# Retention and a gated MLP in one kernel: q loaded four tokens to a partition, w_in as float32 by SyncE's queue, an engine listed per cast

## The chip, the cores and the metric

One core of a Trainium2 chip. TensorE (PE) multiplies and writes to PSUM, VectorE (DVE), ScalarE (ACT) and GpSimd (POOL) do the elementwise work, SyncE (SP) issues transfers between HBM and SBUF, which run on the core's 16 DMA engines. The metric is the device time of one execution in microseconds (us), lower is better. A profiled execution has in addition a span: from the first to the last instruction that the profile shows.

## The reference

Eight batches, eight heads, 576 positions, head size 64. Retention (attention without softmax, with a decay for each head), then an MLP over the 512 joined features whose V half is normed, mixed over positions by a 576 x 576 matrix and multiplied onto the U half:

```python
scores = scale * np.matmul(q, k.transpose(0, 1, 3, 2))
gamma = 1.0 - 2.0 ** (-5.0 - np.arange(H))
Dmat = np.where(rel >= 0, gamma[:, None, None] ** rel[None, :, :], 0.0)
x = np.matmul(scores * Dmat, v)          # (B, H, S, D), then joined to (B, S, 512)

h = gelu_tanh(x @ w_in)                  # w_in: 512 x 1024
u, v = h[..., :512], h[..., 512:]
v_n = (v - mean(v)) / np.sqrt(var(v) + 1e-06) * g_ln
v_s = np.einsum('ts,bsd->btd', w_sg, v_n) + b_sg[None, :, None]
return x + (u * v_s) @ w_out
```

Everything enters and leaves as float32; the kernel multiplies in bfloat16.

## The kernel before

Two batches make a pair p of 1152 tokens. For attention a pair is nine tiles n (`U = 9`, 36 in all): four heads by 256 tokens of one batch each, but for the middle one (`MID` = 4), which holds all heads of 64 tokens of each batch. For the MLP a pair is nine tiles m of 128 tokens.

A tile of attention goes so. `load` (line 311) brings its q, k and v as float32 into one of six buffers (`qkf`, `vf`), by SyncE's queue, 256 KB a load; a row of SBUF gets two neighbouring tokens of each head, so 512 bytes run together in HBM. The middle tile takes two loads of 128 KB for each of q, k and v. `scaled` (504) casts k to `kb`, multiplies q by the decay into `qs` and v by its inverse into `vb`, all bfloat16. `turned` (541) transposes q and k on PE (8 matmuls, L547) and copies them from PSUM to `qkT`. `score` (566, L572) multiplies q by k, `mask` (576) puts the triangle on and writes `ret`; `states` (596, L605) multiplies k by v into running states, which `keep` (626) adds up in float32 (`s1`, `s2`, `zmid`) and casts to `zsA` and `zsB`. `outp` (678, L692) adds the products of q with the states and of `ret` with v, and writes `xT`, features by tokens. For tiles from the twentieth on, q and k are transposed by DMA (L499).

The MLP takes `xT`: `mlp_V` (815, L821, 4 matmuls of 512 columns) needs the V half of `w_in`, its gelu and statistics follow, then `norm` writes `vn`; `mlp_U` (857, L868) needs the U half. `batch` (878) does the mixing with w_sg (L890), the product with U (L898) and the out projection (L923), which adds x by identity matmuls (L926) or, in the last 18 tiles, from a DMA transpose.

`w_load` (338) brings `w_in` in four pieces, each half of the rows by half of the columns, through GpSimd's own queue; that DMA casts to bfloat16 on the way. It stands in GpSimd's program between its casts and products. The first two pieces are V's, the others U's. `weights` (447) loads w_sg, casts it on GpSimd, transposes it on PE and copies it to `wT` (and, shifted by 64 partitions, `wT1`); `w_out` follows.

The order of the whole program is a list: the table `TURN` holds for every unit of work (by the name of what it writes, in the order of `plan.add`) its place, and `Plan.emit` issues the units in that order, each on its engine. An engine runs its instructions in that order and waits at each for what it needs. `Plan.emit` reckons times from each unit's `cost` for two things only: which PSUM bank a unit takes, and where PE is given matmuls on zeros (`fill`, L301) to keep it busy, up to 45 us. Transfers of SyncE's queue take turns at eight semaphores, and each waits until the one eight earlier has landed.

Of the kernel before, what the change touches and what calls it, by code (L numbers as in the profile page):

```python
# [11 lines left out]
F32 = mybir.dt.float32  # L12
# [7 lines left out]
    "b_col": [57],  # L20
    "b_rows": [0, 58],
    "b_tr": [72],
    "dtab": [33],
# [4 lines left out]
    "g_col": [76],  # L28
    "g_col1": [89],
    "g_inv": [90],  # L30
    "g_rows": [21, 109],
    "g_tr": [121],
    "gelu": [51],
# [6 lines left out]
    "ident": [4],  # L40
# [12 lines left out]
    "otu": [48, 55, 92, 110, 136, 162, 197, 268, 304, 335, 377, 419, 447, 472, 498, 539, 554, 582, 610, 640, 673,  # L53
        703, 718, 751, 782, 823, 839, 883, 914, 946, 969, 1004, 1026, 1053, 1068, 1101],
# [32 lines left out]
        807, 810, 945, 922, 940, 928, 1019, 1065, 1046, 1044, 1066, 1143, 1120, 1149, 1147],  # L87
    "wT": [244, 247, 273, 239, 276],
    "wT1": [326, 327, 293, 370, 287],
    "wT_b": [74],  # L90
    "wTp": [238, 237, 272, 233, 275],
    "w_in": [25, 38, 100, 82],
    "w_out": [320, 298, 333, 331],
# [923 lines left out]
```

## Time and profile before

| | us |
|---|---|
| median of 3 runs | 209.04 (207.84 to 210.18) |
| the profiled execution | 209.62 |
| its span | 207.9 |
| first U product of w_in (L868) starts | 29.33 |
| first mixing product (L890) starts | 50.38 |
| last matmul ends | 203.1 |

The page gives busy time by engine, the span in 40 slices, DMA queues, the chain of work that ended last, and groups of instructions by line. `out<-in` names the tiles; "128*128" is the part of PE's array in use, "128x512" partitions by elements. In a timeline each row is a start, a length, the engine, and in brackets how long the engine sat idle before it and what it waited for. SyncE's loads keep the DMA engines busy nearly all the time: over the span they moved 48.20 MB in 98321 packets, 90.0% of 16 engines' span on SyncE's queue and 3.6% on GpSimd's.

### The profile page before, as it was taken

Reading aid. Unit: us, or ns where it says so; the run is one execution under the profiler, and the core shown is the slowest. Engines: PE = TensorE matmul, PEld = TensorE weight load, DVE = VectorE, ACT = ScalarE, POOL = GpSimd, SP = SyncE. Lnnn points to the kernel's source line nnn. Section 1 sums busy time; section 2 is a strip of 40 time slices with the busy share of each in tenths; the row PEclk is TensorE's granted clock in tenths of the full one; section 3 lists DMA queues with packets and bytes.
Section 4 is the critical chain, followed back from the end, with each engine's and each line's share of the span. In section 5 each row is a group of like instructions: output and inputs, shape, how many; then the busy total and the mean of one; then the engine's idle time right before and its main releaser. Section 6 shows DMA issues by size and latency. Waiting matters only on the chain.

```text
span 207.9 us, 7429 instructions
## 1 busy us (share of the span) xinstructions
PE 194.2 (93%) x2994; PEld 124.2 (60%) x3027; DVE 150.8 (73%) x366; ACT 134.7 (65%) x316; POOL 135.8 (65%) x231
## 2 busy tenths in 40 slices
PE   6977949999999999999999999999999999999992
PEld 2543536768767776567745666575656565664651
DVE  1654953998987888978786658575869689896672
ACT  5363325799999846788589776765777377826400
POOL 6557989489769996759779865749846866123200
PEclk9999966999999999999999999999999999999999
DMA  5999999999999998695999899998998999895815
GB/s 145 267 203 192 228 274 302 300 296 309 192 277 251 290 330 213 175 241 136 265 210 299 229 175 199 271 317 208 255 267 236 201 175 262 192 189 195 249 54 202
DMA packets 98321, 48.20 MB, mean 232 GB/s; under 512 B 42288, under 2 KB 92720, under 8 KB 98288
## 3 DMA queue, kind: packets, MB, share of 16 engines
q1 hardware_dynamic: 97056, 46.56, 90.0%
q0 software_dynamic: 1088, 1.05, 3.6%
q8 instruction: 23, 0.38, 0.8%
q10 hardware_dynamic: 144, 0.13, 0.2%
q14 instruction: 10, 0.08, 0.1%
HBM read 32.79 MB, written 9.44 MB: 203 GB/s over the span
## 4 chain that ended last, share of the span: by engine, by line
PE 85%; DMA 8%; POOL 2%; issue 2%; DVE 1%; SPq 0%; DVEq 0%; POOLq 0%
PE p_d L890 19%; PE p_d L868 16%; PE p_d L923 14%; PE p_d L821 14%; PE p_oz L692 7%; PE p_d L547 4%; DMA w_in<-in_moe_w_in_dram 4%; PE p_s L572 3%; DMA vf<-in_v_dram 3%; PE p_d L926 2%; DMA qkf<-in_q_dram 1%; PE p_oz L605 1%; PE p_d L301 1%; PE p_d L460 1%; POOL vb L537 1%
## 5 line engine op out<-in xcount | busy, mean ns | idle before, releaser
L586 DVE TENSOR_TENSOR ret<-p_s,tri 128x512 bf16<-128x512 f32 x64 | 42.5, 681 | 3.2 <-PE p_s L572 3.0
L537 POOL TENSOR_TENSOR vb<-vf,gv 128x512 bf16<-128x512 f32 x36 | 37.6, 1046 | 6.9 <-DMA vf<-in_v_dram 6.0
L890 PE MATMUL p_d<-wT,vn 128*128 128x288 bf16 x256 | 40.5, 286 | 0.0
L868 PE MATMUL p_d<-xT,w_in 128*128 128x512 bf16 (+2 forms) x224 | 37.9, 314 | 2.1 <-DMA w_in<-in_moe_w_in_dram 2.1
L534 POOL TENSOR_TENSOR qkb<-qkf,gq 128x512 bf16<-128x512 f32 x35 | 36.5, 1047 | 4.3 <-DMA qkf<-in_q_dram 2.8
L821 PE MATMUL p_d<-w_in,xT 128*128 128x512 bf16 x126 | 34.8, 380 | 1.3 <-issue 0.5
L923 PE MATMUL p_d<-w_out,uT 128*128 128x512 bf16 (+1 forms) x137 | 34.5, 373 | 0.9 <-issue 0.5
L898 DVE TENSOR_TENSOR uT<-p_d,uT 128x288 bf16<-128x288 f32 x64 | 27.6, 448 | 6.1 <-PE p_d L890 4.8
L890 PEld LDWEIGHTS <-vn 128*128 128x128 bf16 x256 | 24.4, 98 | 7.1
L873 ACT ACTIVATE uT<-p_d 128x512 bf16<-128x512 f32 x36 | 21.2, 596 | 11.1 <-PE p_d L868 11.0
L853 ACT ACTIVATE vn<-vg,stat 128x512 bf16<-128x512 f32 x32 | 25.6, 814 | 3.8 <-POOL stat L840 3.7
L868 PEld LDWEIGHTS <-w_in 128*128 128x128 bf16 x224 | 19.4, 101 | 13.6 <-DMA w_in<-in_moe_w_in_dram 2.3
L838 POOL TENSOR_TENSOR stat<-stat,mhalf 128x1 f32<-128x1 f32 x36 | 20.2, 562 | 11.0 <-DVE stat L832 6.0
L824 ACT ACTIVATE vg<-p_d 128x512 f32<-128x512 f32 x36 | 20.9, 596 | 9.3 <-PE p_d L821 9.2
L829 DVE BATCH_NORM_STATS2 stat<-vg 128x6 f32<-128x512 f32 x36 | 24.6, 684 | 2.5 <-ACT vg L824 2.4
L530 POOL CAST qkb<-qkf 128x512 bf16<-128x512 f32 x32 | 19.5, 613 | 8.5 <-DMA qkf<-in_k_dram 5.8
L550 DVE COPY qkT<-p_d 128x1024 bf16<-128x1024 bf16 x20 | 13.7, 683 | 11.7 <-PE p_d L547 11.5
L923 PEld LDWEIGHTS <-uT 128*128 128x128 bf16 x148 | 13.7, 98 | 13.1
L821 PEld LDWEIGHTS <-xT 128*128 128x128 bf16 x144 | 13.0, 98 | 12.2 <-DVE xT L772 0.4
L837 POOL TENSOR_SCALAR stat<-stat 128x1 f32<-128x1 f32 x26 | 5.6, 217 | 20.7 <-DVE stat L830 15.6
L890 PE MATMUL p_d<-wT,vmid 128*128 128x288 bf16 x64 | 18.4, 287 | 0.0
L547 PE MATMUL p_d<-ident,qkb 128*128 128x128 bf16 x160 | 13.3, 229 | 1.0 <-POOL qkb L534 0.8
(103 smaller groups left out, 308.3 us busy)
## 6 DMA issues: line engine op xcount, KB each, us to landing
out_dram<-ob SPq DMA_DIRECT2D x35, 256.0 KB, 3.9
qkf<-in_q_dram SPq DMA_DIRECT2D x32, 256.0 KB, 5.4
qkf<-in_k_dram SPq DMA_DIRECT2D x32, 256.0 KB, 5.5
vf<-in_v_dram SPq DMA_DIRECT2D x32, 256.0 KB, 5.6
wsg<-in_moe_w_sg_dram SPq DMA_DIRECT2D x4, 288.0 KB, 5.1
w_in<-in_moe_w_in_dram POOLq DMA_DIRECT2D x4, 256.0 KB, 5.7
qkf<-in_k_dram SPq DMA_DIRECT2D x8, 128.0 KB, 5.1
qkf<-in_q_dram SPq DMA_DIRECT2D x8, 128.0 KB, 5.0
```

Of the source, the lines that this page charges most:

```text
L534: plan.add("POOL" if i else "DVE", 1010 if i else 700, key, lambda: eng.tensor_tensor(split(qs[a]), shape(qkf[l][:, 0, :]), gain(gq), op=A ...
L537: plan.add("POOL", 1010, key + 2, lambda: nc.gpsimd.tensor_tensor(shape(vb[a][:]), shape(vf[l][:]), gain(gv), op=Alu.mult), reads=rd(i, 2) ...
L547: nc.tensor.transpose(banks[0][:].bitcast(BF)[:, (x * KK + kk) * 128:(x * KK + kk + 1) * 128], src[:, kk * 128:(kk + 1) * 128], ident[:])
L586: nc.vector.tensor_tensor(ret[r][x][:].rearrange("p (s k j) -> p s k j", s=2, k=2), banks[0][:].rearrange("p (s k) j -> p s k j", s=2), tr ...
L821: nc.tensor.matmul(banks[0][:], xT[p % NX][:, m, kk, :], w_in[:, kk, F2:], start=(kk == 0), stop=(kk == KK - 1))
L829: nc.vector.bn_stats(st[:, 0:6], vg[g][:])
L853: nc.scalar.activation(vn[p % 2][m][:], vg[g][:], Act.Identity, scale=st[:, 8:9], bias=st[:, 9:10])
L868: nc.tensor.matmul(hu[:, c, :].rearrange("p (t j) -> p t j", j=128), w_in[:, kk, 128 * (x * per + c):128 * (x * per + c) + 128], xT[p % NX ...
L873: plan.add("ACT", 500, key, lambda banks, x=x: nc.scalar.activation(uT[p % NX][:, x * per:x * per + per, cols], banks[0][:].rearrange("p ( ...
L890: nc.tensor.matmul(banks[0][:, :HS], src[:, 128 * c:128 * c + 128], wT[e][j][:, half * HS:(half + 1) * HS], start=(j == 0), stop=(j == SB ...
L898: plan.add("DVE", 380, key, lambda banks, c=c, col=col: nc.vector.tensor_tensor(uT[x][:, c, col:col + HS], banks[0][:, :HS], uT[x][:, c, c ...
L923: nc.tensor.matmul(banks[0][:, :w], uT[x][:, c, r], w_out[:, c, x0:x0 + w], start=(c == 0), stop=late and c == KK - 1, skip_group_check=True)
```

## The change

q is loaded with four neighbouring tokens to a partition (`QS = 4`), which is 1 KB in a run; to have two heads beside each other as before, a tile's q comes in two loads of 128 KB, each onto 64 partitions. The decay table for q (`gq`) is built for that layout, with its logarithms in a small table `lnr`; the triangle, the columns of q in `q_cols` and the writes to `xT` follow it (steps of four tokens instead of two). The number of loads on SyncE's queue rises by one a tile.

`w_in` comes through SyncE's queue as float32, in four pieces of 256 columns and all 512 rows, into buffers of the output (`obs`) and one of its own (`wst`), and is cast by ACT (V's two pieces) or GpSimd (U's). A U product needs only the piece that holds its columns; the first two V tiles are computed in two halves of 256 columns (`hv`, `hw`).

Casts, products and copies that may run on either of two engines are listed in `SIDE`, a letter each. And `TURN` is another order for everything.

```diff
-    POOLED = 10
+    POOLED, QS = 10, 4
...
+SIDE = {
+    "kb": "APAPPPPAAPPPPPPAPAPPPPPAAPPPPPAPPPPP",
+    "qkT": "DDDAAAADDAADDADADADD",
+    "qs": "DDPPPDPPDPPPPPPPPPPPPPPPPPPPPPPPPPPP",
+    "vb": "PPPDPDDPDPPPDPPPPPPDPPPPPPPDPDDPPPPD",
+    "wT": "DDDAD",
+    "wT1": "APPPP",
+    "w_in": "AAPP",
+    "wnat": "PPPPP",
+    "zbdA": "PPPPPPPPPAPPPAAPAAAPAPPPAPAA",
+    "zbdB": "--PAAAAA--PAPAAA--AAAPPA--AAPAPP",
+}
...
 TURN = {
-    "hv": [73, 66, 150, 142, 195, 231, 229, 345, 329, 411, 425, 492, 473, 531, 566, 563, 630, 633, 688, 671, 732,
+    "hv": [90, 97, 135, 131, 187, 280, 265, 386, 367, 434, 440, 523, 499, 536, 640, 573, 638, 666, 721, 723, 762,
...
+                if not a:
+                    for y in range(2):
+                        plan.add("SP", 400, i * T0 - 4 * T0 + a,
+                                 lambda dst=dst, e=e, r0=r0, c=c, y=y: nc.sync.dma_start(
+                                     dst[64 * y:64 * y + 64, :].rearrange("p (r f) -> p r f", r=2),
+                                     q[2 * p + e, c * HU + y:c * HU + HU:2, r0:r0 + 256, :].rearrange("r (g s) d -> g r (s d)", s=QS)),
+                                 writes=[("ld", 0, l, y)], dma=390)
+                    continue
...
     def w_load(half, c):
-        plan.add("POOL", 770, (1 - half) * T0 + 10 + c, lambda: nc.gpsimd.dma_start(
-            w_in[:, c:c + 2, half * F2:(half + 1) * F2],
-            moe_w_in.rearrange("(c p) f -> p c f", p=128)[:, c:c + 2, half * F2:(half + 1) * F2]),
-            reads=[("ld", 1, 0, 0)] if half else [("vb", 1)], writes=[("w_in", half, c), ("w_in", half, c + 1)], dma=1500)
+        x = 2 * (1 - half) + c
+        part_ = wst[:] if x == 3 else obs[x][:].rearrange("p a f -> p (a f)").rearrange("p (k f) -> p k f", k=KK)
+        held = [] if x == 3 else [("ob", 2 * x), ("ob", 2 * x + 1)]
+        f0 = half * F2 + c * (F2 // 2)
+        plan.add("SP", 450, (1 - half) * T0 + 10 + c, lambda: nc.sync.dma_start(
+            part_, moe_w_in.rearrange("(k p) f -> p k f", p=128)[:, :, f0:f0 + F2 // 2]),
+            writes=[("wf", x)] + held, dma=1550)
+        plan.add({"ACT": 965, "POOL": 985}, None, (1 - half) * T0 + 10 + c, lambda e: copy(
+            e, w_in[:, :, f0:f0 + F2 // 2], part_),
+            reads=[("wf", x)] + held, writes=[("w_in", half, c)])
...
-        plan.add("DVE", 600, key, lambda banks: nc.vector.tensor_copy(
-            qkT[r][:].rearrange("p a k c -> p (a k c)"), banks[0][:].bitcast(BF)),
+        plan.add({"DVE": 600, "ACT": 915}, None, key, lambda e, banks: copy(
+            e, qkT[r][:].rearrange("p a k c -> p (a k c)"), banks[0][:].bitcast(BF)),
...
-        return qkT[r][rows, 0, 2 * k:2 * k + 2, EA[e]]
+        w = 128 // QS
+        return qkT[r][rows, 0, :, 64 * k + w * e:64 * k + w * e + w]
```

What the order makes of it shows at three places. In these rows `qkf_61` to `qkf_66` and `vf_67` to `vf_72` are the six buffers (tile 0 is in 61 and 67, tiles 1 and 2 in 62 and 68, 3 in 61 and 67 again, 4 in 63 and 69, 5 in 64 and 70, 6 in 65 and 71, 7 in 66 and 72), `ob_144` to `ob_146` the output's buffers.

The U half of w_in, before: GpSimd's program from v of tile 2 on. Its two DMAs stand between products.

```order
L537 TENSOR_TENSOR vb_77<-vf_68,gv 128x512
L339 DMA w_in<-in_moe_w_in_dram 128x2x512
L537 TENSOR_TENSOR vb_78<-vf_67,gv 128x512
L672 CAST zsA_95<-s_1_94 128x128
L401 TENSOR_SCALAR g_tmp<-g_col 128x4
L402 TENSOR_SCALAR g_inv<-g_col 128x4
L403 TENSOR_TENSOR g_tmp<-g_tmp,g_inv 128x4
L404 TENSOR_TENSOR g_col<-g_col,g_tmp 128x4
L339 DMA w_in<-in_moe_w_in_dram 128x2x512
```

After, SyncE's queue from q of tile 5 on, with the two U pieces (L388) behind k and behind v of tile 6:

```order
L366 DMA qkf_64<-in_q_dram 64x2x256
L366 DMA qkf_65<-in_q_dram 64x2x256
L372 DMA vf_70<-in_v_dram 128x4x128
L366 DMA qkf_65<-in_q_dram 64x2x256
L372 DMA qkf_65<-in_k_dram 128x4x128
L388 DMA ob_146<-in_moe_w_in_dram 128x4x256
L372 DMA vf_71<-in_v_dram 128x4x128
L388 DMA wst<-in_moe_w_in_dram 128x4x256
```

and GpSimd's program from q and k of tile 6 (`qkf_65`) on, where the casts of both pieces (L340) stand ahead of q of tile 7:

```order
L588 TENSOR_TENSOR qkb_74<-qkf_65,gq 128x2x4x64
L340 CAST qkb_74<-qkf_65 128x2x4x64
L893 TENSOR_TENSOR stat_121<-stat_121,mhalf 128x1
L340 CAST zsA_95<-zmid_89 128x256
L340 CAST w_in<-ob_146 128x4x256
L340 CAST w_in<-wst 128x4x256
L588 TENSOR_TENSOR qkb_74<-qkf_66,gq 128x2x4x64
```

The U half has moved from GpSimd's queue to the end of the loads for tile 6 on SyncE's.

On PE, before, the first U product (L868) comes after the output of tile 3 (L692), the scores (L572) and states (L605) of the middle tile and the transposes of g (L423); equal rows are shown once:

```order
L692 MATMUL p_oz<-ret_1_88,vb_78 64x128
L572 MATMUL p_s_167<-qkT_79 64x64
L605 MATMUL p_d_172<-vb_75,qkb_73 64x64
L423 MATMUL p_d_173<-ident,g_rows 128x128
L868 MATMUL p_d_171<-xT_99,w_in 128x256
```

After, it (L923) comes behind the transposes of tile 6 (L601), a V product (L872) and the output of tile 5 (L740):

```order
L740 MATMUL p_oz<-ret_1_82,vb_75 64x64
L627 MATMUL p_s_171<-qkT_79 64x128
L660 MATMUL p_d_175<-vb_76,qkb_73 64x64
L601 MATMUL p_d_176<-ident,qkb_74 128x128
L872 MATMUL p_d_173<-w_in,xT_99 128x512
L740 MATMUL p_oz<-ret_1_84,vb_76 64x128
L923 MATMUL p_d_175<-xT_99,w_in 128x256
```

Ahead of the first U product there are now seven tiles' transposes instead of five, six tiles' scores and states instead of five, six outputs instead of four, and five V products instead of two.

More of the change, by code (lines that the diff above doesn't have):

```diff
@@ L92 @@
[L92 to L94 removed]
[5 rows of a table removed]
[L100 removed]
[8 rows of a table removed]
[L109 to L113 removed]
+    "b_col": [61],
@@ L128, with __init__ @@
     FIRST = {"PE": 1300, "DVE": 900, "ACT": 2100, "POOL": 500, "SP": 350}
-    def __init__(self, pools, turn, fill):
+    def __init__(self, pools, turn, side, fill):
         self.units = []
+        self.sides = {}
+        self.side = side
         self.fill = fill
@@ L141, in add @@
         mine = self.seen[name] = self.seen.get(name, -1) + 1
+        if isinstance(engine, dict):
+            sides, some = engine, emit
+            self.sides[len(self.units)] = sides
+            engine = self.side[name][mine] if name in self.side else next(iter(sides))
+            engine = {e[0]: e for e in sides}[engine[0]]
+            cost, emit = sides[engine], lambda *banks: some(engine, *banks)
         self.look[len(self.units)] = look
@@ L303, with copy @@
     xr_turn = [0]
-    plan = Plan({"s": p_s, "oz": [p_oz], "d": p_d}, TURN, fill)
+    plan = Plan({"s": p_s, "oz": [p_oz], "d": p_d}, TURN, SIDE, fill)
+    by = {"POOL": nc.gpsimd, "DVE": nc.vector}
+    def copy(e, dst, src):
+        if e == "ACT":
+            nc.scalar.activation(dst, src, Act.Copy)
+        else:
+            by[e].tensor_copy(dst, src)
     T0 = 5300.0
@@ L870, in mm @@
                                          start=(kk == 0), stop=(kk == KK - 1), skip_group_check=True)
[L871 removed]
+            u = plan.add("PE", 900 if w == 128 else 880 if w == 256 else 870, key, mm, reads=[r for m in ms[::2] for r in x_reads(p, m)] + [("w_in", 0, c) for c in range(x * per * 2 // KK, (x * per + per - 1) * 2 // KK + 1)],
                          writes=[("hu", p, ms[0], x)], take=[("d", 1)])
@@ L973 @@
         if not i:
-            for c in (0, 2):
+            for c in range(2):
                 w_load(1, c)
@@ L980 @@
         if i == 1:
-            for c in (0, 2):
+            for c in range(2):
                 w_load(0, c)
```

226 lines of the change are left out of this document (117 added, 109 removed), and 108 rows, old and new, of the table TURN.

## The prediction

> **What bounds the kernel now.** I read the page's first two parts, then the chain of waits in order of time. On the page: busy time of an engine with its share, and below it 40 slices of 5.2 us with the busy tenths.
>
> ```profile
> PE 194.2 (93%) x2994; PEld 124.2 (60%) x3027; DVE 150.8 (73%) x366; ACT 134.7 (65%) x316; POOL 135.8 (65%) x231
> PE   6977949999999999999999999999999999999992
> PEclk9999966999999999999999999999999999999999
> DMA  5999999999999998695999899998998999895815
> ```
>
> PE is nearly full from the seventh slice on and loose before it, with the granted clock at 0.6 in slices six and seven. So there are two stages: a start that waits for loads, and a long stretch that PE bounds. The chain (start, length in us, what) shows where one turns into the other:
>
> ```profile
> 0.79 3.10 DMA qkf<-in_q_dram
> ...
> 8.03 0.25 PE p_d L605 x16
> ...
> 21.84 7.45 DMA w_in<-in_moe_w_in_dram
> 29.33 3.60 PE p_d L868 x16
> 32.92 0.85 PE p_d L547 x8
> ...
> 38.91 0.98 PE p_d L868 x8
> 39.89 0.45 PE p_d L547 x8
> ...
> 41.20 0.46 PE p_oz L692 x24
> ...
> 42.63 0.35 PE p_s L572 x16
> ...
> 79.55 0.86 PE p_d L821 x4
> ...
> 117.72 0.32 PE p_oz L692 x24
> ```
>
> The last load that PE waits for is the U half of w_in: issued at 21.84, landed at 29.33, when the first U product (L868) starts. The windows (us, busy per engine with counts, granted clock, DMA share, GB/s) price the two sides:
>
> ```profile
> 4.00:8.00 4.00, 3.68 (x34) 1.53 (x35) 1.35 (x3) 1.43 (x9) 2.30 (x3) 1.00 0.99 268
> 20.00:24.00 4.00, 3.70 (x75) 2.07 (x74) 3.67 (x11) 2.05 (x5) 3.67 (x9) 1.00 1.12 211
> 24.00:28.00 4.00, 2.49 (x62) 1.47 (x59) 3.90 (x12) 1.42 (x4) 3.86 (x9) 0.95 1.12 232
> 28.00:32.00 4.00, 2.67 (x13) 1.94 (x14) 0.74 (x3) 0.60 (x1) 3.10 (x6) 0.50 1.15 307
> 32.00:36.00 4.00, 3.95 (x74) 2.60 (x74) 1.39 (x4) 1.96 (x6) 4.00 (x7) 0.70 1.04 307
> 44.00:48.00 4.00, 3.95 (x55) 2.46 (x54) 3.47 (x11) 3.87 (x9) 4.00 (x7) 1.00 1.08 323
> 28.00:200.00 172.00, 168.50 (x2642) 110.83 (x2672) 131.28 (x319) 121.82 (x273) 115.94 (x188) 0.98 0.97 239
> ```
>
> From 28 to 200 us PE is idle for 172.0 - 168.5 = 3.5 us only. What can be won is therefore how much of PE's work is done before the first U product, when that starts, and at which clock. The profiled execution took 209.62 us (span 207.9, 1.7 around it); the median of the three runs is 209.04, 0.6 below it.
>
> **The change, part by part.** *Work put ahead of the U half.* By the order of PE, ahead of the first U product now stand, more than before: two transposes of q and k (0.45 each by the row at 39.89), scores (0.35) and states (0.25) of one tile, the output of the middle tile (0.32) and of tile 5 (0.46), and three V products (0.86 each by the row at 79.55). 0.90 + 0.35 + 0.25 + 0.32 + 0.46 + 2.58 = 4.9 us that no longer follow it. Below 29 us they cost nothing, since PE waits there: in the timeline of PE (start, length, idle before it)
>
> ```profile
> 26.82 0.40 PE L423 MATMUL p_d<-ident,g_rows 128*128 128x128 bf16 x4
> 29.33 3.60 PE L868 MATMUL p_d<-xT,w_in 128*128 128x256 bf16 x16 [2.11 <-DMA w_in<-in_moe_w_in_dram]
> ```
>
> nothing stands between 27.2 and 29.3. -4.9.
>
> *The cold stretch behind that wait.* The 16 products at 29.33 took 3.60, where eight later took 0.98: 3.60 - 1.96 = 1.6 lost; the transposes at 32.92 took 0.85 against 0.45: 0.4 lost. The clock rows (0.50, 0.70) fit. With work ahead of U and no idle stretch as long, -2.0; between 0 (it goes cold again) and -2.0, and I take -2.0, as PE now has the 4.9 us above to run in that stretch.
>
> *When the U half is there.* It now comes by SP's queue, behind the loads of tiles 0 to 3, 4, 5, q and k of tile 6 and both V pieces. The nearest event before with as much ahead of it is v of tile 5, for which POOL waits (timeline of POOL):
>
> ```profile
> 29.98 1.04 POOL L537 TENSOR_TENSOR vb<-vf,gv 128x512 bf16<-128x512 f32 x1 [0.90 <-DMA vf<-in_v_dram]
> ```
>
> The issues (count, KB each, us to landing):
>
> ```profile
> qkf<-in_q_dram SPq DMA_DIRECT2D x32, 256.0 KB, 5.4
> w_in<-in_moe_w_in_dram POOLq DMA_DIRECT2D x4, 256.0 KB, 5.7
> qkf<-in_k_dram SPq DMA_DIRECT2D x8, 128.0 KB, 5.1
> qkf<-in_q_dram SPq DMA_DIRECT2D x8, 128.0 KB, 5.0
> ```
>
> Ahead of it, and with it, lay five full tiles (15 x 256 KB), the middle tile (6 x 128 KB) and w_in, 512 KB a piece in float32 in HBM (the row counts its bfloat16): 3.75 + 0.75 + 2.0 = 6.5 MB. Up to the first U piece now: q and k of six tiles (12 x 256 KB), v of five, the middle tile, three pieces: 3.0 + 1.25 + 0.75 + 1.5 = 6.5 MB. The same, so 29.98 again, with two corrections. Rows of 1 KB for q: 512-byte loads alone ran at 268 GB/s (4 to 8 us), with the 2,304-byte rows of w_sg among them at 307; 1.5 MB of q gain 0 to 0.7 us, and I take 0.7. Nothing beside the small loads: SP waits for the eighth load before the one it issues, eight loads of 128 KB that land in 5.0 us are 210 GB/s (the row 20 to 24 has 211), and w_in no longer fills in from POOL's queue. Some 1 MB at 210 instead of 255 GB/s (6.5 MB in 29.98 us less the 3.1 that the first load takes): 0.9 later, between 0 and 0.9. So it lands at 30.2. Then POOL's cast, 1,024 elements a partition. The nearest rows (groups of instructions: count, busy, mean ns):
>
> ```profile
> L537 POOL TENSOR_TENSOR vb<-vf,gv 128x512 bf16<-128x512 f32 x36 | 37.6, 1046 | 6.9 <-DMA vf<-in_v_dram 6.0
> ...
> L530 POOL CAST qkb<-qkf 128x512 bf16<-128x512 f32 x32 | 19.5, 613 | 8.5 <-DMA qkf<-in_k_dram 5.8 <-PE p_oz L605 2.6
> ...
> L550 DVE COPY qkT<-p_d 128x1024 bf16<-128x1024 bf16 x20 | 13.7, 683 | 11.7 <-PE p_d L547 11.5
> ...
> L534 DVE TENSOR_TENSOR qkb<-qkf,gq 128x512 bf16<-128x512 f32 x1 | 0.7, 719 | 0.4 <-DMA qkf<-in_q_dram 0.4
> ```
>
> Two casts of 613 ns, 1.2 us; between 0.6 and 2.3 (behind a product of 1,046 first). First U product at 31.4 instead of 29.3: +2.1, bounds -0.2 and +3.8. The second piece is wanted four groups later (0.98 + 0.35 + 0.25 + 0.98 = 2.6 us), and stands 0.75 MB (2.9 us at 255) behind the first: +0.3 at most, left out.
>
> *The Trainium skill on half the partitions.* Each q load now fills 64 partitions. "DMA: Bandwidth & Descriptors", sections "Where 436 GB/s comes from" and "The descriptor swizzle", has 16 SBUF ports as the bottleneck, with half the partitions behind half of them (told of software descriptors). The rows neither show nor exclude it: the loads onto 64 partitions above took 5.0 us for half the bytes. By the page q would run at half pace; its own result is a rival below.
>
> *Casts and copies by list.* DVE takes 13 of q's and v's products (719 ns) and gives up 9 qkT copies (683): +3 us on 150.8. POOL gives up those 13 and 5 casts of k, and takes two w_in casts, four wT copies and 19 small state casts: about 6 us less. ACT:
>
> ```profile
> L735 ACT ACTIVATE xT<-p_oz 128x256 bf16<-128x256 f32 x24 | 11.0, 458 | 4.5 <-PE p_oz L692 2.4 <-PE p_d L890 0.9 <-DVE s L666 0.6
> L752 ACT ACTIVATE xs<-p_oz 128x256 f32<-128x256 f32 x24 | 9.1, 379 | 4.9 <-PE p_oz L692 2.0 <-DVE stat L829 1.3 <-PE p_oz L605 1.2
> L657 ACT ACTIVATE zsB<-s 128x128 bf16<-128x128 f32 x24 | 7.4, 306 | 4.7 <-DVE s L652 4.6
> L476 ACT ACTIVATE wT<-wT 64x1152 bf16<-64x1152 bf16 x3 | 3.5, 1162 | 0.1
> L528 ACT ACTIVATE qkb<-qkf 128x512 bf16<-128x512 f32 x4 | 2.5, 630 | 7.3 <-DMA qkf<-in_k_dram 7.3
> ```
>
> gains 9 qkT copies (1,024 elements, between 630 and 1,162 ns; 1.05), 5 casts of k (0.63) and two of w_in (1.1), 14.8 us, and loses 21 small state casts (0.31), four wT copies (4,608 elements in all, 4.6 by the 1,162 for 1,152) and a put of wT (0.6), 12 us: +3 on 134.7. It sits under PE, which is full; where ACT is full too (3.87 of 4 us from 44 to 48) it loses the wT copies. 0, between -2 and +3. Writing xT in steps of four tokens instead of two: dense xs takes 379 ns, stepped xT 458; 0 to 79 ns for 32 evictions, 2.5 us of ACT off the path, 0 on it.
>
> *Next to be late.* w_sg: 3.4 MB stand behind the first U piece, and the last of it lands 3.4 / 0.307 = 11.2 us later, is cast 0.7 later (613 ns for 512 elements, 576 here), and PE comes to its transposes after 11.4 us of other products (seven U groups at 0.98 or a little less, two V products, the rest attention, by the rows above): +0.5, between 0 and the 4.1 of the rival below.
>
> Sum: -4.9 - 2.0 + 2.1 + 0.5 = -4.3. 209.62 - 4.3 = 205.3 for an execution like the profiled one, 204.7 from the median: I say 204.9. By the bounds of U's arrival the likeliest case runs from 202.6 to 206.6.
>
> **The rivals.** *Half pace of q, and cold again.* As a mechanism of this kernel: each 128 KB half takes as long as 256 KB does now. 1.5 MB of q ahead of the U half cost 6 us more if the halves run one after the other, none if both halves of a tile are under way together; in four of six tiles they stand side by side, so 2 to 3. PE then waits over 2 us ahead of U as before, and the 2.0 of cold clock return: 204.9 + 2.5 + 2.0 = 209.4, no change. For it: the row 28 to 32 shows a clock of 0.50 after a 2.1 us wait. Against: eight loads are in flight, so halves meet.
>
> *The gain is given back at w_sg.* If the loads behind U run at the 232 GB/s of the row 24 to 28, w_sg is late by 3.4 / 0.232 + 0.7 - 11.4 = 4.0 instead of 0.5: 208.4, no change either. For it: that row. Against: both rows in which w_sg came show 307.
>
> *Slower: ACT in the path of each tile.* Nine tiles now wait for ACT, in whose queue the copy stands behind evictions, between their transposes and their scores. All 14.8 us added, none of the 12 removed counting: 219.7. Over 211.1 from 6.2 us on, under half of it; for a price of 8, 212.9. For it: ACT's 3.87 of 4 us. Against: most of these tiles lie where ACT is busy for 2.05 (20 to 24) or 0.60 (28 to 32) of 4 us.
>
> **How the numbers follow.** Likeliest 0.67 (204.9), w_sg 0.10 (208.4), half pace 0.14 (209.4), slower 0.09 (212.9). About 1% is what a measurement of this kernel can tell from no change: faster is below 206.95, slower above 211.1. Faster: 0.67 and a part of w_sg's, 0.69; the same 0.22; slower 0.09. The range leaves out the slower case, what half pace gives above 209.4, and a little of the likeliest below its bounds: 201.8 to 209.4.
>
> **What would show it.** Right: the first product of w_in's U columns at 30 to 32 us with five V products before it, its eight matmuls in about 1 us, and PEclk at 9 in slices six and seven. Wrong: an idle PE of over 2 us ahead of it (half pace: q to landing well above 5.0), w_sg's cast releasing PE's transposes, or PE idle over 5 us from 32 us on with ACT as releaser. The w_in cast on POOL over 2 us would move the sum by as much.

## The result, and the profile after

The changed kernel is slower: 226.28 us median of four runs (223.88 to 227.11), against 208.94 on the same chip; the ratio is 1.081, 95% interval 1.071 to 1.091. The forecast was 204.9, with 209.4 as the upper end. The profiled execution has a span of 224.6 us.

The page of the changed kernel, busy time by engine and the slices (now 5.6 us each):

```profile
PE 195.2 (87%) x2994; PEld 123.8 (55%) x3026; DVE 160.9 (72%) x389; ACT 145.9 (65%) x304; POOL 131.7 (59%) x238
PE   7559967998999976999997997999599999999993
PEclk9997999999999999999999999999999999999999
DMA  4999799997998898799989999979999999585265
```

PE has the same work (195.2 against 194.2 us) and more idle time: 224.6 - 195.2 = 29.4 us against 13.7. The idle time isn't in one place; slices with a 7 or less stand all along the PE row. The chain of work that ended last says who is waited for, before and then in the changed kernel:

```profile
PE 85%; DMA 8%; POOL 2%; issue 2%; DVE 1%; SPq 0%; DVEq 0%; POOLq 0%
```

```profile
PE 34%; DMA 30%; SPq 14%; POOL 6%; ACT 6%; DVE 4%; issue 3%; DVEq 0%; POOLq 0%; ACTq 0%
```

DMA has risen from 8% of it to 30%, and SP's queue from nothing to 14%. In the windows (us, busy per engine, granted clock, DMA share, GB/s) the cold clock between 28 and 36 us is gone, as forecast (the PEclk row now has a 7 in its fourth slice instead), but from 28 to 200 us PE is idle for 172.0 - 153.1 = 18.9 us instead of 3.5:

```profile
28.00:32.00 4.00, 2.24 (x69) 1.61 (x70) 3.61 (x12) 3.59 (x9) 2.37 (x4) 1.00 0.86 244
32.00:36.00 4.00, 2.49 (x39) 1.60 (x40) 2.08 (x6) 2.48 (x4) 2.38 (x4) 1.00 1.08 315
28.00:200.00 172.00, 153.09 (x2516) 99.55 (x2543) 127.89 (x299) 121.17 (x250) 111.74 (x184) 1.00 0.97 232
```

The first U product, in PE's timeline, comes at 35.23 instead of 29.33 (31.4 was forecast), behind GpSimd's cast of w_in; its eight matmuls take 1.05 us, so they are not cold. In GpSimd's timeline that cast waits for its piece of w_in to land; the prediction had the landing at 30.2 and 1.2 us for the cast:

```profile
33.86 0.39 PE L740 MATMUL p_oz<-ret,vb 64*64 64x128 bf16 x16
35.23 1.05 PE L923 MATMUL p_d<-xT,w_in 128*128 128x256 bf16 x8 [0.97 <-POOL w_in L340]
```

```profile
34.13 1.04 POOL L340 CAST w_in<-ob 128x1024 bf16<-128x1024 f32 x1 [0.80 <-DMA ob<-in_moe_w_in_dram]
```

Ahead of it, in the timeline of SP (start, length, what was issued):

```profile
24.23 1.24 SPq L366 DMA_DIRECT2D qkf<-in_q_dram  x2
25.52 0.59 SPq L372 DMA_DIRECT2D vf<-in_v_dram  x1
26.16 0.60 SPq L366 DMA_DIRECT2D qkf<-in_q_dram  x1
26.80 0.59 SPq L372 DMA_DIRECT2D qkf<-in_k_dram  x1
27.44 0.51 SPq L388 DMA_DIRECT2D ob<-in_moe_w_in_dram  x1
```

Each row begins where the last one ended: SP waits for nothing, and issues as fast as it can, one load in 0.5 to 0.6 us, while the DMA share in the row 28 to 32 is down to 0.86. The piece of w_in that the U product needs is not issued before 27.44. The rows of the q loads, of the changed kernel (count, ns min/median/max):

```profile
L366 SPq DMA_DIRECT2D qkf<-in_q_dram x64: 595/602/1817, 0.8 to 168.7; - x64
```

and of the kernel before, a full tile's load onto 128 partitions, then the middle tile's onto 64:

```profile
L327 SPq DMA_DIRECT2D qkf<-in_q_dram x32: 368/512/3310, 0.8 to 154.2; - x32
```

```profile
L319 SPq DMA_DIRECT2D qkf<-in_q_dram x8: 601/822/1617, 16.4 to 134.9; - x8
```

A load onto 64 partitions never takes SP under 595 ns, for half the bytes; onto 128 it can be 368, though the medians of these rows, 602 to 822 against 512, lie closer together. The lengths of all of SP's issues, added up, were 163.1 us of 207.9 before and are 180.4 of 224.6 now. Up to the end of the issue of the last load of q, k or v they fill 138.6 of 165.1 us before (84%) and 158.4 of 179.5 us now (88%): that last load goes out 14.4 us later, and the span is 16.7 us longer. Who waits late in the changed kernel, in the groups of instructions:

```profile
L591 POOL TENSOR_TENSOR vb<-vf,gv 128x512 bf16<-128x512 f32 x26 | 27.0, 1043 | 17.0 <-DMA vf<-in_v_dram 15.4 <-PE p_d L660 1.4
...
L783 ACT ACTIVATE xT<-p_oz 128x256 bf16<-128x256 f32 x24 | 17.9, 744 | 2.5 <-DVE s L703 1.1 <-PE p_oz L740 1.0 <-DVE s L719 0.3
L815 DVE TENSOR_TENSOR xT<-p_oz,xs 128x256 bf16<-128x256 f32 x24 | 17.5, 728 | 7.1 <-ACT xT L783 7.0
L340 POOL CAST qkb<-qkf 128x512 bf16<-128x512 f32 x27 | 16.4, 611 | 20.7 <-DMA qkf<-in_k_dram 19.7 <-DMA qkf<-in_q_dram 0.5 <-ACT vn L908 0.4
```

GpSimd waits 15.4 us for v and 19.7 for k, where it waited 6.0 and 5.8. And the second suspect shows in the same rows: an eviction into xT takes 744 ns on ACT and 728 on DVE, where it took 458 and 440.

In what follows a time is the median of all executions of a run while its ratio leaves out the disturbed ones, of which after_step2_tiny128 had three in four, so that it has no interval and stands with the 218.51 us of its undisturbed one.

### The profile page after: what moved, and what is told of

Its sections match the earlier page's. It is cut to its first block, busy times and chain, and to the rows that moved or that the text cites. A ratio compares the mean times of both kernels' runs of the same rounds, so it can differ in the third digit from the quotient of the medians.

```text
span 224.6 us, 7543 instructions
## 1 busy us (share of the span) xinstructions
PE 195.2 (87%) x2994; PEld 123.8 (55%) x3026; DVE 160.9 (72%) x389; ACT 145.9 (65%) x304; POOL 131.7 (59%) x238
## 4 chain that ended last, share of the span: by engine, by line
PE 34%; DMA 30%; SPq 14%; POOL 6%; ACT 6%; DVE 4%; issue 3%; DVEq 0%; POOLq 0%; ACTq 0%
DMA qkT<-qkb 9%; PE p_d L945 9%; DMA qkf<-in_q_dram 8%; PE p_d L978 8%; PE p_d L923 6%; DMA vf<-in_v_dram 5%; SPq L366 5%; PE p_d L872 4%; SPq L356 4%; DMA qkf<-in_k_dram 3%; DMA ob<-in_moe_w_out_dram 3%; SPq L372 3%; PE p_oz L740 3%; POOL vb L591 2%; POOL qkb L588 2%
## 5 line engine op out<-in xcount | busy, mean ns | idle before, releaser
L923 PE MATMUL p_d<-xT,w_in 128*128 128x512 bf16 (+2 forms) x224 | 36.5, 303 | 1.5 <-POOL w_in L340 1.4
L591 POOL TENSOR_TENSOR vb<-vf,gv 128x512 bf16<-128x512 f32 x26 | 27.0, 1043 | 17.0 <-DMA vf<-in_v_dram 15.4
L872 PE MATMUL p_d<-w_in,xT 128*128 128x512 bf16 (+1 forms) x139 | 35.9, 367 | 1.1 <-ACT vg L879 0.3
L588 POOL TENSOR_TENSOR qkb<-qkf,gq 128x512 bf16<-128x512 f32 x28 | 29.0, 1042 | 9.8 <-DMA qkf<-in_q_dram 8.4
L340 POOL CAST qkb<-qkf 128x512 bf16<-128x512 f32 x27 | 16.4, 611 | 20.7 <-DMA qkf<-in_k_dram 19.7
L879 ACT ACTIVATE vg<-p_d 128x512 f32<-128x512 f32 x36 | 21.6, 604 | 7.5 <-PE p_d L872 7.2
L923 PEld LDWEIGHTS <-w_in 128*128 128x128 bf16 x224 | 18.5, 98 | 12.4 <-POOL w_in L340 1.8
L815 DVE TENSOR_TENSOR xT<-p_oz,xs 128x256 bf16<-128x256 f32 x24 | 17.5, 728 | 7.1 <-ACT xT L783 7.0
L872 PEld LDWEIGHTS <-xT 128*128 128x128 bf16 x152 | 13.7, 98 | 12.0 <-DVE xT L815 0.9
L601 PE MATMUL p_d<-ident,qkb 128*128 128x128 bf16 x160 | 13.6, 224 | 7.7 <-POOL qkb L340 3.9
L783 ACT ACTIVATE xT<-p_oz 128x256 bf16<-128x256 f32 x24 | 17.9, 744 | 2.5 <-DVE s L703 1.1
L627 PE MATMUL p_s<-qkT 64*64 64x128 bf16 (+1 forms) x576 | 14.4, 218 | 4.6 <-DMA qkT<-qkb 4.2
```

The costliest lines, as they stand in the source:

```text
L588: plan.add({"POOL": 1000, "DVE": 620}, None, key, lambda e: by[e].tensor_tensor(split(qs[a]), shape(qkf[l][:, 0, :]), gain(gq), op=Alu.mul ...
L591: plan.add({"POOL": 1000, "DVE": 620}, None, key + 2, lambda e: by[e].tensor_tensor(shape(vb[a][:]), shape(vf[l][:]), gain(gv), op=Alu.mul ...
L872: nc.tensor.matmul(banks[0][:, y * w:y * w + w], xT[p % NX][:, m, kk, :], w_in[:, kk, F2 + y * w:F2 + y * w + w], start=(kk == 0), stop=(k ...
L879: plan.add("ACT", 500, key, lambda banks: nc.scalar.activation(vg[g][:], banks[0][:], Act.Gelu_apprx_tanh), reads=[("hv", i), ("hw", i)], ...
L923: nc.tensor.matmul(hu[:, c, :].rearrange("p (t j) -> p t j", j=128), w_in[:, kk, 128 * (x * per + c):128 * (x * per + c) + 128], xT[p % NX ...
```

## The experiments

Three theories. *Queue*: the second q load of each tile costs SP's time, and all loads come late. *Stride*: the step of four in xT makes each tile's eviction 0.57 us longer, on the way that frees p_oz. *Order*: the new order, or the engine list, loses the time by itself. Ratios are to the kernel before on the same chip, with 95% intervals.

**after_step2.** The changed kernel with two tokens a partition and two loads of 128 KB:

```diff
-    POOLED, QS = 10, 4
+    POOLED, QS = 10, 2
-  dst[64*y:64*y+64, :]  <- q[.., c*HU+y:c*HU+HU:2, r0:r0+256, :]  "r (g s) d -> g r (s d)"
+  dst[64*y:64*y+64, :]  <- q[.., c*HU:c*HU+HU, r0+128*y:r0+128*y+128, :]  "h (p s) d -> p h (s d)"
```

> The changed kernel with q laid out two tokens a partition again (xT written in steps of two), but q still in two loads of 128 KB onto 64 partitions each; order, engine list and w_in as changed. Stride theory (xT written in steps of four makes the eviction of each tile some 0.29 us longer on ACT and again on DVE, on the way that frees p_oz): the 24 full tiles give 24 x 0.57 = 13.7 us back, 210 to 214 us. Queue theory (SP issues 32 more loads, each 0.60 us, and they come late): the same number of issues remains, so 222 to 227 us. Order theory (the new order and engine list lose the time): 222 to 227 us.

228.05 us, 1.098 (1.089 to 1.107). The stride theory falls: with the evictions back in steps of two nothing came back.

**after_step2_one_load.** The same with one load of 256 KB a tile:

```diff
-  for y in range(2): two loads onto 64 partitions
+  dst[:]  <- q[.., c*HU:c*HU+HU, r0:r0+256, :]  "h (p s) d -> p h (s d)"
```

> As the run with two tokens a partition, and q in one load of 256 KB a tile as before the change: 32 issues fewer on SP. Stride theory: no better than the run with two loads, 210 to 214 us. Queue theory: this run alone recovers the time, 208 to 213 us, where the one with two loads stays at 222 to 227. Order theory: still 220 to 227 us.

210.54 us, 1.017 (1.009 to 1.025): without the 32 second loads the ratio falls from 1.098 by 0.081. Its first U product, in PE's timeline, starts where the prediction had it for the changed kernel, and SP issues the piece of w_in for it 3.3 us earlier than at 27.44:

```profile
31.36 1.05 PE L914 MATMUL p_d<-xT,w_in 128*128 128x256 bf16 x8
```

```profile
24.11 0.81 SPq L388 DMA_DIRECT2D ob<-in_moe_w_in_dram  x1
```

**before_step4.** The kernel before with q alone changed:

```diff
-    POOLED = 10
+    POOLED, QS = 10, 4
+TURN["ld"]: the second q load of a tile right behind the first
```

> The kernel before with q alone changed: four tokens a partition in two loads of 128 KB, xT written in steps of four; the second load stands right behind the first in SP's order, all else in the order and on the engines of before, w_in by GpSimd's queue. Stride theory: 209 + 13.7 = 219 to 224 us. Queue theory: 32 issues of 0.60 us more on SP, of which the waits of SP hide a part: 213 to 224 us, with the first U product late. Order theory: 208 to 211 us.

220.22 us, 1.063 (1.054 to 1.072). q's new layout alone brings most of the loss into the old order; the order theory falls with it.

**before_w_in_f32.** The kernel before with w_in alone changed:

```diff
-  nc.gpsimd.dma_start(w_in[:, c:c+2, half*F2:(half+1)*F2], ...)
+  nc.sync.dma_start(part_, ...); copy(e, w_in[:, :, f0:f0+F2//2], part_)
```

> The kernel before with w_in alone changed: float32 column pieces by SP's queue at the places where GpSimd issued them, V cast by ACT, U by GpSimd right ahead of their first products. Stride theory and order theory: 207 to 212 us. Queue theory: four issues more on SP between the loads of tiles 3 to 6, each about 0.5 us, and two casts of 1.04 us on GpSimd ahead of U: 210 to 214 us.

210.01 us, 1.014 (1.006 to 1.022): some 2.9 us, within what both theories had. w_in by SP has a price of its own; four issues more on SP and the casts are not told apart.

**after_step2_by_heads.** Two loads of 128 KB still, but each onto 128 partitions:

```diff
-  dst[64*y:64*y+64, :]          <- four heads of 128 tokens
+  dst[:, 256*y:256*y+256]       <- two heads of 256 tokens
```

> As the run of the changed kernel with two tokens a partition and two loads of q a tile (228.05 us), but the two loads are split by heads: each is 128 KB onto all 128 partitions instead of 64. The count of loads and their bytes are the same. Count theory (each load more takes SP's time and one of the eight places in flight, whatever its shape): 222 to 229 us. Half-partition theory (a load onto 64 partitions is slow itself, in its issue or in its landing): most of the 17.5 us to the run with one load comes back, 210 to 215 us.

214.70 us, 1.027 (1.015 to 1.038). The count and the bytes are those of the 228.05; of the 0.081 that one load gave back, 0.071 came back with the form alone. SP's row for these loads:

```profile
L366 SPq DMA_DIRECT2D qkf<-in_q_dram x64: 378/486/2399, 0.8 to 157.1; - x64
```

**after_step2_tiny and after_step2_tiny128.** One load a tile, and beside it a load of 8 KB that nobody waits for, onto 64 partitions in the one, onto 128 in the other:

```diff
+  nc.sync.dma_start(tiny[i % 4][:], q[.., c*HU:c*HU+2, r0:r0+64, :16])    # after_step2_tiny
+  nc.sync.dma_start(tiny[i % 4][:], q[.., c*HU:c*HU+2, r0:r0+128, :8])    # after_step2_tiny128
```

> As the run of the changed kernel with two tokens a partition and one load of q a tile (210.54 us), with one more load in the place of each second q load that nobody waits for: 64 partitions, two pieces of 64 bytes each, 8 KB, 32 of them. Count theory: slow again, 222 to 229 us, though 0.26 MB are moved more. Half-partition theory, if it is the landing of 128 KB on half the partitions: 209 to 213 us; if it is the issue of the 64-partition form (0.60 us against 0.37 to 0.51): between, 215 to 225 us.

> As the run with 32 small loads that nobody waits for (226.12 us), but each of them goes onto 128 partitions (two pieces of 32 bytes each) instead of 64: the same 8 KB, the same count, the same places in flight, the same order. If it is SP's time for the 64-partition form (0.595 us at least, against about 0.37 for 128 partitions): half or more of the 15.6 us over the run with one load goes, 212 to 219 us. If the count of loads or the eight places in flight do it: 223 to 229 us.

226.12 us, 1.086 (1.076 to 1.097), with 64 partitions: 32 loads of 8 KB cost nearly as much as the real halves (1.098), so it isn't the landing of 128 KB on half the partitions. Nor is it the eight places in flight: SP's waits for an earlier landing, added up from its wait rows, are 3.9 us with these loads and 4.5 without them. With 128 partitions 218.51, which is 1.047 by that one execution: less than half of the rise from 1.017 to 1.086 is left. SP's rows, of the first kernel and of the second:

```profile
L371 SPq DMA_DIRECT2D tiny<-in_q_dram x32: 595/622/2069, 0.8 to 169.4; - x32
```

```profile
L371 SPq DMA_DIRECT2D tiny<-in_q_dram x32: 368/506/1979, 0.8 to 162.9; - x32
```

So both count: that there is an issue more, and that its form takes SP longer. How they share the loss is less sure, as the run on 128 partitions rests on one execution.

**before_split.** The kernel before with q in two loads onto 64 partitions, two tokens and steps of two:

```diff
+  for y in range(2): dst[64*y:64*y+64, :]  <- q[.., r0+128*y:r0+128*y+128, :]
```

> The kernel before with q in two loads of 128 KB onto 64 partitions each and nothing else changed: two tokens a partition, xT in steps of two. SP's-time theory: as with four tokens a partition (220.22 us), 217 to 222 us. Theory that the step of four is a good part of that run's loss: 209 to 215 us.

218.86 us, 1.048 (1.038 to 1.057): the split alone is most of before_step4's 6.3%.

**before_evict_step4.** The kernel before, only its evictions in steps of four:

```diff
-  xT[..] "p n k (j s) -> p (n k) s j", s=2  <- oz "p e (b s j) -> p (e b) s j", s=2
+  xT[..] "p n k (j s) -> p (n k) s j", s=4  <- oz "p e (b s j) -> p (e b) s j", s=4
```

> The kernel before, its loads and its order untouched, with the evictions of p_oz written into xT in steps of four instead of two (128x256: ACT 458 to about 744 ns, DVE 440 to about 728 by the rows of the changed kernel); tokens inside a block come out permuted, no work is left out. Stride theory: 24 x 0.57 = 13.7 us on the path, 218 to 224 us. Theory that TensorE covers them: at most what the run with split and step of four has over the run with the split alone (1.5%), 207 to 212 us.

210.54 us, 1.005 (1.001 to 1.010). Its evictions are as long as the changed kernel's, in the groups by form:

```profile
L735 ACT ACTIVATE xT<-p_oz 128x256 bf16<-128x256 f32 x24 | 17.8, 742 | 4.4 <-PE p_oz L692 2.2 <-PE p_d L890 0.9 <-DVE s L666 0.7
```

24 x 0.57 = 13.7 us of longer evictions cost about 1 us. The rest is hidden; the next run bears out that PE hides it.

**before_natural.** The other way around, q's columns read by PE in token order and xT written without a step:

```diff
-  qkT[r][rows, 0, 2*k:2*k+2, EA[e]]
+  qkT[r][rows, 0, 2*k:2*k+2, EA[e]].rearrange("p s g -> p g s")
```

> The kernel before, with q's columns read by TensorE in the order of tokens (its moving operand has a step there), so that p_oz holds tokens in order and xT is written without a step. Evictions of xT on ACT 458 to about 380 ns (the row of xs) and on DVE 440 to about 380. Stride theory in its form for the path: 24 x 0.14 = 3 us less, 203 to 205 us. Theory that these evictions are covered while loads are in time: no difference, 206 to 208 us. A step in TensorE's moving operand that costs: p_oz and p_s products above 218 ns, 208 to 214 us.

217.75 us, 1.050 (1.042 to 1.058). The evictions fell to 380 ns as expected, and bought nothing; the scores, by form, went from the first row (before) to the second:

```profile
L572 PE MATMUL p_s<-qkT 64*64 64x128 bf16 x512 | 12.8, 217 | 0.2
```

```profile
L571 PE MATMUL p_s<-qkT 64*64 64x128 bf16 x512 | 21.2, 282 | 0.1
```

PE's busy time rose by 9.5 us (203.7 against 194.2), and the time by 10.5. What PE gets to do more, the kernel takes longer; what ACT and DVE get, it hides.

**after_q_128.** The changed kernel with each of its two loads onto 128 partitions, heads 2y and 2y + 1 in 1 KB rows:

```diff
-  dst[64*y:64*y+64, :]     <- q[.., c*HU+y:c*HU+HU:2, ..]     "r (g s) d -> g r (s d)"
+  dst[:, 256*y:256*y+256]  <- q[.., c*HU+2*y:c*HU+2*y+2, ..]  "x (g s) d -> x g (s d)"
```

> The changed kernel as it is (four tokens a partition, xT written in steps of four, two loads of q a tile with rows of 1 KB, w_in by SP, its order and engine list), except that each of the two loads goes onto all 128 partitions (two heads' pieces of 64 partitions each) instead of 64. Theory that SP's time to issue the 64-partition form (0.60 us against 0.37 to 0.51) is the cause: as the run split by heads, 212 to 217 us. Theory that the count of loads is the cause, or the step of four: 222 to 228 us.

339.22 us, 1.626 (1.612 to 1.640): none of the theories. The page of the changed kernel, then of this run:

```profile
DMA packets 91667, 49.27 MB, mean 219 GB/s; under 512 B 42800, under 2 KB 86064, under 8 KB 91632
```

```profile
DMA packets 90771, 49.27 MB, mean 146 GB/s; under 512 B 41904, under 2 KB 85168, under 8 KB 90736
```

896 packets fewer, all of them under 512 B, are 14 for each of the 64 loads. Each load ends with one packet of 4 bytes per DMA engine that took part, so these had 2 engines instead of 16, and the pattern of their source is led by the two heads. The Trainium skill says this in "DMA: Bandwidth & Descriptors", section "Why a DMA increments its semaphore by 16 and not by 1": the number of engines is the largest up to 16 that divides the slowest dimension of both sides. The trace agrees, with 2. The run tells nothing of the issue's price.

**after_q_act and after_q_pool.** The changed kernel with the second q load of each tile issued by ACT's queue, and by GpSimd's:

```diff
-  nc.sync.dma_start(
+  (nc.scalar if y else nc.sync).dma_start(      # after_q_act
+  (nc.gpsimd if y else nc.sync).dma_start(      # after_q_pool
```

> The changed kernel as it is, with the second q load of each tile issued by ACT's queue instead of SP's, at the same place in the order: the loads, their form and the eight places in flight stay, SP has 32 issues of 0.60 us less (19 us), ACT as much more (its busy time was 146 of 225 us). SP's-time theory: 209 to 217 us. Theory that the landing on half the partitions or the eight places in flight are the cause: 222 to 230 us.

> The changed kernel as it is, with the second q load of each tile issued by GpSimd's queue instead of SP's, at the same place in the order; in ACT's queue they had stood behind ACT's waits at the start, and shared the eight places in flight with SP. SP's issues then take some 21 us less than in the changed kernel (180.4 us by the lengths in its trace). SP's-time theory: the runs so far stand at spans of 206, 212, 217, 224 and 227 us for 163, 172, 178, 185 and 188 us of SP's issues, so 206 to 214 us, a little more if GpSimd's 32 issues (about 0.8 us each, 25 us on 132 busy) come into the way. Theory that the landing on half the partitions or the number of loads under way is the cause: 222 to 230 us.

230.77 us, 1.105 (1.095 to 1.115), and 236.96 us, 1.135 (1.124 to 1.146). Both missed: the first lies at the upper end of what the rival theory had, the second above it. A load that stands in another engine's program waits for what that engine waits for. In ACT's timeline of the first (the idle time before a row in brackets) two loads are issued only at 13.21 and 14.10, behind a wait of 4 us:

```profile
13.21 0.20 ACT L1033 ACTIVATE warm<-mhalf 128x4 f32<-128x4 f32 x1 [4.05 <-DVE b_col L429]
13.21 0.61 ACTq L366 DMA_DIRECT2D qkf<-in_q_dram  x1
```

and in GpSimd's timeline of the second a product waits 6.6 us for a q that it had issued itself:

```profile
15.95 0.61 POOL L366 DMA_DIRECT2D qkf<-in_q_dram  x1
16.57 0.62 POOL L340 CAST qkb<-qkf 128x512 bf16<-128x512 f32 x1
23.79 1.04 POOL L588 TENSOR_TENSOR qkb<-qkf,gq 128x512 bf16<-128x512 f32 x1 [6.60 <-DMA qkf<-in_q_dram]
```

The first mixing products came at 60.28 and 69.64 us instead of 52.95. From there on the two took 167.0 and 166.6 us, the changed kernel 171.7, after_step2_one_load 158.6: some 5 of 13 us came back behind the start, and why the other 8 did not isn't shown. One lead is on record for the first: SP's own waits for an earlier landing rose from 8.3 us in the changed kernel to 27.3. The Trainium skill, "Perfetto Trace Analysis", section "DMA Optimizations", says that balancing transfers over the engines that can issue them may help when making their descriptors is the bottleneck; here that lost more than it saved.

**after_one_load.** So the issues were taken away without moving them: the changed kernel as it is, step of four included, with one load of q a tile.

```diff
-  for y in range(2): dst[64*y:64*y+64, :]  <- ...
+  dst[:]  <- q[.., c*HU:c*HU+HU, r0:r0+256, :]  "h (p s) d -> p h (s d)"
```

> The changed kernel as it is (step of four in xT, order, engine list, w_in by SP as float32), but q comes in one load of 256 KB onto 128 partitions a tile, as before the change: 32 issues fewer on SP, the same bytes. The products and evictions run as in the changed kernel; q's values then stand at other tokens than the rest of the kernel takes them for, so the output is not the reference's. Theory that the second load's issue on SP is the cause: as the run with two tokens and one load (210.54 us) and about 1 us for the step (before_evict_step4 had 0.5%), 208 to 214 us. If something else in the layout of four tokens does it: 218 to 227 us.

211.17 us, 1.011 (1.004 to 1.017). Of the 17.3 us all but some 2 are gone. SP issues its last load of q, k or v by 162.0 us instead of 179.5. GpSimd's waits fell with it:

```profile
L591 POOL TENSOR_TENSOR vb<-vf,gv 128x512 bf16<-128x512 f32 x26 | 27.3, 1060 | 10.7 <-DMA vf<-in_v_dram 9.0 <-PE p_oz L740 1.6
...
L340 POOL CAST qkb<-qkf 128x512 bf16<-128x512 f32 x27 | 16.4, 610 | 9.0 <-DMA qkf<-in_k_dram 5.6 <-PE p_oz L660 3.3
```

**after_step2_w_in_pool and after_order_only.** Two tokens, one load, and w_in by GpSimd again: order, engine list and the halved V products are left. In the first the planner, which reckons with GpSimd's transfer, put 99 products on zeros into PE (25.7 us) instead of 29 (10.7); the second keeps them near the latter.

```diff
-  plan.add("POOL", 770, ..., lambda: nc.gpsimd.dma_start(w_in[...]), dma=1500)
+  plan.add("SP", 0, ..., lambda: nc.gpsimd.dma_start(w_in[...]))       # after_order_only
```

> As the run of the changed kernel with two tokens a partition and one load of q a tile (210.54 us), with w_in by GpSimd's queue again in four pieces of rows that it converts itself: what is left of the change is the order, the engine list and the V products of two tiles in two halves. If w_in as float32 by SP is what is left of the loss (the kernel before with w_in alone changed had 1.4% more): 206 to 208 us, no difference to before. If the order or the engine list loses: 209 to 212 us. If they gain what was forecast for the work ahead of U: 201 to 205 us.

> The changed kernel with two tokens a partition, one load of q a tile, and w_in by GpSimd's queue, as the run of 218.22 us, but with the zero products that the planner puts into TensorE's waits as in the run with one load (about 33 instead of 99). If those 66 zero products (25.7 against 10.7 us of TensorE) were its loss: 204 to 209 us. If GpSimd's queue brings w_in late in this order whatever is filled in: 214 to 219 us.

218.22 us, 1.049 (1.039 to 1.060), and 209.39 us, 1.003 (0.998 to 1.008). With about as many products on zeros as in the changed kernel, the order and the list together neither gain nor lose. It is the best of the versions with the new order, and no run beat the kernel before.

The sums of SP's issues, worked out from each trace, rise with the spans but for before_step4 (before_split is faster with 4 us more of issues). Beside them stands the time at which the last issue for q, k or v ends:

| run | SP's DMAs | sum of their issue times, us | last load issued, us | span, us |
|---|---|---|---|---|
| after_step2_one_load | 188 | 162.8 | 159.7 | 206.1 |
| before | 184 | 163.1 | 165.1 | 207.9 |
| after_one_load | 188 | 166.5 | 162.0 | 208.8 |
| after_step2_by_heads | 220 | 172.2 | 167.2 | 212.0 |
| before_step4 | 216 | 174.7 | 173.7 | 220.5 |
| after_step2_tiny128 | 220 | 177.7 | 172.0 | 216.8 |
| before_split | 216 | 178.8 | 173.5 | 217.3 |
| changed kernel | 220 | 180.4 | 179.5 | 224.6 |
| after_step2_tiny | 220 | 184.7 | 179.5 | 224.4 |
| after_step2 | 220 | 187.6 | 181.3 | 227.1 |

In these and in the eight other profiles the span ends 43 to 47 us after that last load is issued. The sums alone do not tell the span: after_q_act and after_q_pool have 150.1 and 160.3 us of SP's issues and spans of 227.3 and 236.2, with the last load at 180.5 and 190.0.

An issue's length may hold time in which SP was held back as well, and a load can go out late because its buffer is not free, so the table by itself shows no cause; the runs that took issues away or added them do.

## Why the prediction was wrong

**The step that failed is "When the U half is there", and with it the whole stretch behind.** It reckoned q's two loads as bytes in a queue: rows of 1 KB, 128 KB in flight instead of 256, a pace in GB/s. It gave SP no time for issuing them. The row that has that time is L319 of the kernel before, loads onto 64 partitions; it was read for its landing (5.0 us) and not for its 601 ns on SP, and nothing of SP's own timeline went into the sum. For the small loads it charged the eight places in flight instead (0.9 us), while SP's rows from 24.23 to 27.95 us wait for no landing. 64 issues at 0.60 instead of 32 at about 0.5 are some 20 us of SP's time in a kernel in which SP already issued for 163 of 208 us. So the U piece landed at 34.13 instead of 30.2, while the cast took 1.04 us of the 1.2 allowed for it. The first U product is late by 3.9 us (35.23 against 31.36 with one load and two tokens; 32.33 with one load and four). That 31.36 meets the forecast of 31.4 is partly luck: that run has neither the rows of 1 KB nor the small loads, whose corrections, -0.7 and +0.9, nearly cancel. And, what the prediction had no term for at all, loads go on coming late up to the last one at 179.5 us: GpSimd waits eight times for each of q, k and v. The experiments show this part: the second loads taken away in the changed kernel bring 1.081 down to 1.011, and 32 loads of 8 KB that nobody waits for bring 1.017 up to 1.086. The Trainium skill, "Perfetto Trace Analysis", section "What "DMA-bound" means", counts an issuing engine whose track is solid with transfers as a bound of its own, apart from the DMA engines; SP's rows from 24.23 to 27.95 us are that.

Two figures of the prediction don't come out of its own terms. With 0.7 gained, nothing lost and 0.6 for the cast the lower bound of U's arrival is +0.6, not -0.2, so the likeliest case begins at 203.4; and 3.4 / 0.307 is 11.1. Neither changes the outcome.

**That PE bounds the stretch from 28 to 200 us** was right for the kernel before (before_natural: 9.5 us more on PE, 10.5 us longer) and did not hold after. PE 98% busy hid that SP was issuing for 84% of the time up to its last load: two limits stood close together, and only one was looked at.

**Work ahead of the U half, -4.9, and the cold stretch, -2.0.** The mechanism came as forecast: five V products ahead, and U products that are not cold (clock 1.00 in both rows). The gain did not last, and this is the second step that failed: even without the second loads the changed kernel stands at 1.011, not at the forecast 0.98. With the order and the list alone (after_order_only) the first U product comes at 32.54, 3.2 us later than before, which leaves 3.7 of the 6.9 us; the first mixing product does start 3.1 us earlier, as these rows of the two timelines show, before and then after_order_only (the 50.38 of the table ahead is from the chain):

```profile
50.21 0.65 PE L890 MATMUL p_d<-wT,vn 128*128 128x288 bf16 x4
```

```profile
47.14 0.65 PE L929 MATMUL p_d<-wT,vn 128*128 128x288 bf16 x4
```

but from there to the end it needs 159.2 us against 157.7, and the ratio is 1.003, with at most 0.2% of gain in its interval. So half of what the start won was given back later, for a reason that stays open. The rest, 1.6 us, can be the choice of the profiled executions: after_order_only's took 208.17 us against its median of 209.39, the kernel before's 209.62 against 209.04.

**w_in by SP** was costed by its arrival and nothing else. In the old order it costs 1.4% (0.6 to 2.2), about 2.9 us; in the new order the two runs that differ by little else, 1.017 and 1.003, lie as far apart. Its parts were not tried apart.

**Casts and copies by list, 0 between -2 and +3**: nothing speaks against it, but the list is in after_order_only together with the order and was not tried alone; the half that was given back may be its price.

**The step of four, 0 to 79 ns an eviction, "2.5 us of ACT off the path, 0 on it".** The place was right, the size was not: the step from two to four costs 286 ns on ACT and 288 on DVE, not what the step from one to two had cost on ACT (79). Off the path it came to 0.5% (0.1 to 1.0). The Trainium skill, "SBUF — State Buffer", section "Door 1: The DMA port swizzle", in a note on cachelines, lets bfloat16 step by up to eight elements within a line of 16 bytes at no cost; for these writes the trace differs, 380 ns without a step (before_natural), 458 at two and 744 at four, and the measurement decides.

**w_sg, +0.5**: about right. In the changed kernel PE's weight loads for its transposes wait 1.0 us for the cast, and the transposes 0.4.

**The rivals.** Half pace of q had the right load and the wrong reason: q's landing was 4.6 us, not above 5.0, and 8 KB onto 64 partitions cost nearly as much as 128 KB. No run here shows the ports of which the Trainium skill's page "DMA: Bandwidth & Descriptors", section "Where 436 GB/s comes from", speaks. The slower rival, ACT in the path of each tile, did not come: ACT waits 3.8 us for PE's transposes there, and PE and its weight loads wait 1.8 us in all for the qkT copies on ACT. The slower side had its chance from the wrong mechanism.

## What to carry to other kernels

Read the timeline of the engine that issues the transfers like that of any other: add up the lengths of its issues, and if they fill most of the time up to its last load, price every transfer more by its issue and its form, however few bytes it moves. Splitting a load in two to get longer runs in HBM has such a price, and moving issues to another engine puts them behind that engine's waits. And where two resources are nearly full, name both before costing a change by one of them.

## What the runs showed of the hardware

An issue on SP took at least 595 ns for a load onto 64 partitions, whether it moved 128 KB or 8 KB, and down to 367 ns onto 128 partitions; the medians for q were 602 to 822 and 486 to 569. On ACT's queue the same form took 602 to 887 ns.

A load whose pattern is led by a dimension of 2 ran on 2 of the 16 DMA engines (after_q_128: 896 packets of 4 bytes fewer for 64 loads), and made the kernel 1.63 times as long.

Reading TensorE's moving operand with an inner step of 256 bytes (before_natural) took a 64x128 product from 217 to 282 ns.

Evictions of 128x256 from PSUM into bfloat16 took 380, 458 and 744 ns on ACT with steps of 1, 2 and 4 elements (before_natural, before, changed kernel), on DVE, which adds `xs`, 417, 440 and 728.
